# Another order of columns in the large matrix products of a linear-attention and softplus kernel

## The chip, the core and the metric

The kernel runs on one core of one Trainium2 chip. The metric is the device time of one execution in microseconds. Before the change the median of three runs is 870.96 us (868.03 to 871.09).

## What is computed

Eight batches of eight heads of linear attention, 576 positions of 64 elements each, are normalised by their root mean square; the heads are put side by side into rows of 512, and a two-layer network with a softplus between its layers works on the 4608 rows.

```python
kv = np.einsum('bhsd,bhse->bhde', k, v)
out = np.einsum('bhsd,bhde->bhse', q, kv)
rms = np.sqrt(np.mean(out * out, axis=-1, keepdims=True) + 1e-06)
x = (out / rms * g_norm)             # rows of 4608 x 512
h = x @ w_in                         # 512 x 2048
g = np.maximum(h, 0.0) + np.log1p(np.exp(-np.abs(h)))
return g @ w_out                     # 2048 x 512
```

## The kernel before

**Numbers in three parts.** TensorE multiplies operands of the type fp32r. To come nearer to fp32 (the inputs are even wider), each operand is split into a high part, a low part and a third made of the two, and each large product is the sum of three matmuls over these parts. So every factor lies in SBUF as three planes, and the loops over `m` in the products run over them.

**TensorE, banks and columns.** A matmul holds a 128x128 block of one operand (the weight load, PEld in the profile) and streams the other past it, column by column; the result is added up in a bank of PSUM (128 partitions of 512 fp32 numbers). The streamed operand is `rhs` in the code, the bank the first argument. In before, both are walked from their first column to their last.

**The work in order.** First the attention: `kv_of` (L691) forms the 64x64 products, `rows` (L715) applies them to q, squares, sums, takes the root (L719, L723) and scales (L727), and transposes the result (L733, L771 for q). The rows go to memory as `x`, and are read again and split (`split`, L635 to L641). Weights are fetched, converted and split by `weight`, `divide` and `split_weight` (L496 to L524). Then, in two manners, the network:

- *Steps* (`step`): the tokens lie in 12 blocks of 384. For each block `n`, 4 (blocks 0 to 3) or 6 (blocks 4 to 11) chunks `c` of 128 of the 2048 inner columns are done this way, 64 steps. `mm1` (L858) makes 12 matmuls of 384 columns, a softplus and a split follow on ScalarE (L880, L882) and VectorE (L869 and the next), and `mm2` (L865) makes 9 matmuls of 512 columns into the sums of three banks.
- *Wide steps* (`wide_step`): the rest of the inner columns, in pairs of chunks, with the tokens in 9 blocks of 512, in two phases: 27 steps in the first (three for each block) and 21 in the second (three for each of blocks 0 to 2, two for each of blocks 3 to 8), 48 in all. The first layer is done as seven products of sums and differences of quarter matrices instead of eight. Each product (`product`, L1060) makes 6 matmuls of 256 columns into half a bank; ScalarE copies intermediate sums from half bank to half bank (L1101, L1105), and a VectorE addition (L1109) and softplus (L1087) follow. A split on ScalarE and VectorE (L1117, L1120, L1123) makes the input of `mm2` (L1130): 24 matmuls of 512 columns for each step, in four banks.

Partial results of each phase leave through ScalarE (L925) to memory; in the second phase VectorE adds them into the banks again (L904) before the last products are added there.

**What sets the order.** Every piece of work is a task with an engine, an assumed duration, what it comes after, and which buffers it takes and gives back. `Plan.order` simulates the engines with these durations and writes the tasks down in the order that it finds; each engine then runs its own list in that order. Durations in the plan are constants, so they don't follow from a matmul's access pattern. While TensorE has nothing to do early on, the plan inserts spare matmuls (`warm`, L1224), which multiply the identity by itself; their streamed operand is one 128-column block, read four times:

```python
nc.tensor.matmul(new(s, [P, 4, P]), lhsT=ident_r, rhs=ident_r.unsqueeze(1).to_broadcast([P, 4, P]),
                 start=True, stop=True)
```

Two VectorE operations that the prediction uses turn 32x32 blocks: L746 writes its 512 columns contiguously, and L814 writes runs of 32, the next 96 further on, where three tiles share a buffer.

Of the kernel before, what the change touches and what calls it, by code (L numbers as in the profile page):

```python
# [9 lines left out]
F32R = mybir.dt.float32r  # L10
# [8 lines left out]
P = 128  # L19
# [2 lines left out]
DOWN = 1.0 - 2.0 ** -13  # L22
DOWN_G = 1.0 - 0.99 * 2.0 ** -13
E = 1.0 / RADIX


def shaped(x, shape, dtype):
# [28 lines left out]
class Plan:  # L56
# [19 lines left out]
    def slot(self, ring):  # L76
        return Slot(ring)

    def add(self, engine, ns, run, after=(), pos=0.0, take=(), give=(), size=0, behind=None, follows=None, kind="all"):
        pos, behind = round(pos, 4), None if behind is None else round(behind, 4)  # L80
        t = Task(engine, ns, run, [a for a in after if a is not None], pos, list(take), list(give), size)
        for s in t.give:
            s.readers += 1
        self.tasks.append(t)
        t.follows = follows
        t.behind = behind
        t.kind = kind
        return t
# [113 lines left out]
def kernel(  # L202
# [24 lines left out]
    nc = tc.nc  # L227
# [20 lines left out]
    LAST = 2  # L248
# [53 lines left out]
    pieces = sb.tile([P, 12, PIECE], F32R, name="pieces")  # L302
# [183 lines left out]
    def split_weight(w, part_of, n, dst, ready, pos, of_in, by_pe=False):  # L486
# [28 lines left out]
        def third():  # L515
            nc.scalar.activation(dst.tile[:, 2], d.tile, func=AF.Copy, scale=-E / (1.0 + E))

# [5 lines left out]
        def third_of_bank():  # L523
            nc.scalar.activation(dst.tile[:, 2], bank.tile, func=AF.Copy, scale=-E / (1.0 + E))  # L524

# [318 lines left out]
    def step(s):  # L844
        n, c = ORDER[s]
        cs = CHUNKS[n]
        h, g, gv = slot("h"), slot("g"), slot("gv")
        if c == cs[0]:
            sums[:] = [slot(f"s{i}") for i in range(TB)]
        xv, w_in, w_out = xv_slots[n], w_slots[0, c], w_slots[1, c]  # L850
        mine = list(sums)
        kept = c >= 4

        def mm1():
            hp = new(h, [P, NT])
            for m in range(3 * KD):
                i, kd = divmod(m, KD)
                nc.tensor.matmul(hp, lhsT=w_in.tile[:, i, kd * P:(kd + 1) * P], rhs=xv.tile[:, i, kd],  # L858
                                 start=(m == 0), stop=(m == 3 * KD - 1))

        def mm2(i):
            if c == cs[0]:
                new(mine[i], [P, d_model])
            for m in range(3):
                nc.tensor.matmul(mine[i].tile, lhsT=gv.tile[:, m, i * P:(i + 1) * P], rhs=w_out.tile[:, m],  # L865
                                 start=(c == cs[0] and m == 0), stop=(c == cs[-1] and m == 2))

        def low():
            nc.vector.tensor_tensor(out=gv.tile[:, 1], in0=g.tile, in1=gv.tile.bitcast(F32)[:, 0], op=ALU.subtract)  # L869

        def less():
            f32 = gv.tile.bitcast(F32)
            nc.vector.scalar_tensor_tensor(out=gv.tile[:, 2], in0=f32[:, 1], scalar=-RADIX, in1=f32[:, 0],
                                           op0=ALU.mult, op1=ALU.add)

        a = add("PE", 2100, mm1, x_split[n] + factors_done[0, c] + [m for _, m in mm1s[-1:]] +
                (factors_done[1, ORDER[s - 2][1]] if s > 1 else []), s, [h],
                ([xv] if c == cs[-1] else []) + ([w_in] if s == last_step[c] and c != 4 else []))
        mm1s.append((s, a))
        a = add("ACT", 490, lambda: nc.scalar.activation(new(g, [P, NT]), h.tile, func=AF.Softplus, scale=1.0 + E),  # L880
                [a], s, [g], [h])
        a = add("ACT", 530, lambda: nc.scalar.activation(new(gv, [P, 3, NT], F32R)[:, 0], g.tile, func=AF.Copy, scale=DOWN),  # L882
                [a], s, [gv])
        a = add("DVE", 570, low, [a], s, [], [g])
        a = add("DVE", 570, less, [a], s)
        for i in range(TB):
            a2 = add("PE", 700, lambda i=i: mm2(i), [a] + factors_done[1, c] + [mm2s.get(i)], s + 1.5,
                     [mine[i]] if c == cs[0] else [],
                     [gv] + ([w_out] if s == last_step[c] and not kept else []))
            mm2s[i] = a2  # L890
            if c == cs[-1]:
                leave(0, n * TB + i, mine[i], a2, s + 1.5)
# [145 lines left out]
    def wide_step(k):  # L1038
        ph, n, p = STEPS[k]
        ab, gv = slot("ab"), slot("gvp")  # L1040
        b = starts[k]
# [3 lines left out]
        mine = list(wide_sums)  # L1045
        outs = [w_slots[1, c] for c in (2 * p, 2 * p + 1)]

        def place(q):
            return ab.tile[:, q // 2, q % 2 * HW:(q % 2 + 1) * HW]
# [3 lines left out]
        def product(u, q):  # L1053
            f, i = PRODUCTS[u]
            w = forms[p][f].tile
            dst, v = unit_slots[ph, n, u]
            for m in range(3):
                for kd in range(2):
                    at = i * 2 * P + kd * P
                    nc.tensor.matmul(place(q), lhsT=w[:, m, at:at + P], rhs=dst.tile[:, m, v, kd] if u < 6 else dst.tile[:, m, kd],  # L1060
                                     start=(u == 0 and not m and not kd), stop=(m == 2 and kd == 1), skip_group_check=True)

        def multiply(u, q, after, pos, take=(), follows=None):
            f = PRODUCTS[u][0]
            give = [unit_slots[ph, n, u][0]] if last else []
            if final and u in (2, 3, 5, 6):
                give.append(forms[p][f])
            return add("PE", 710, lambda: product(u, q), unit_done[ph, n, u] + forms_done[p][f] + list(after), pos, take, give,
                       follows=follows)
# [3 lines left out]
        def gt(dtype=F32):  # L1073
            if dtype not in held:
                held[dtype] = sb.tile([P, 2, WIDE], dtype, tag=f"g{gv.place}", name=f"g{gv.place}_{dtype == F32}")
            return held[dtype]

        def gvt(m, dtype=F32):
            y = gv.tile[:, m]
            return y if dtype == F32R else y.bitcast(F32)  # L1080
# [5 lines left out]
        def softplus(dst, src):  # L1086
            nc.scalar.activation(dst, src, func=AF.Softplus, scale=1.0 + E)  # L1087

        def begin():
            new(ab, None)  # L1090
            product(0, X)
# [33 lines left out]
        def mm2(c, i):  # L1125
            fresh = first and not c and ph < LAST
            if fresh:
                new(mine[i], [P, d_model])
            for m in range(3):
                nc.tensor.matmul(mine[i].tile, lhsT=(gvt(m, F32R) if m < 2 else gt(F32R))[:, c, i * P:(i + 1) * P], rhs=outs[c].tile[:, m],  # L1130
                                 start=fresh and not m, stop=(last and c == 1 and m == 2), skip_group_check=True)

        seeds = {}
# [19 lines left out]
        for c in range(2):  # L1153
            for i in range(TW):
                slot_pos = b + PACE + MM2[TW * c + i]
                a2 = add("PE", 700, lambda c=c, i=i: mm2(c, i),
                         [split_done[c]] + factors_done[1, 2 * p + c] + ([seeds[i]] if i in seeds and not c else []) +
                         ([before[i]] if c or not first else []), slot_pos, [mine[i]] if first and not c and ph < LAST else [], [gv] + ([outs[c]] if final else []))
                before[i] = a2
                if last and c:  # L1160
                    leave(ph, TW * n + i, mine[i], a2, slot_pos)
# [3 lines left out]
    def whole_scale(pos):  # L1165

        if not wide:
            scale_done.append(add("DVE", 60, lambda: nc.vector.memset(scale, 1.0 + E), (), pos))
            return
# [5 lines left out]
        scale_done.append(add("ACT", 200, lambda: nc.scalar.activation(  # L1175
            scale, total.tile[:, 0, :1], func=AF.Copy, scale=(1.0 + E) * 2.0 ** -30 / (P * 2 * KF * d_model)), [a], pos, [], [total]))

# [82 lines left out]
```

## Time and profile before

| what | value |
|---|---|
| median of three runs (lowest, highest) | 870.96 us (868.03, 871.09) |
| span of the profiled execution, first to last instruction | 867.5 us |
| TensorE busy | 853.9 us, 98%, 6464 matmuls |
| VectorE busy | 704.4 us, 81% |
| ScalarE busy | 521.3 us, 60% |
| GpSimd busy | 76.6 us, 9% |
| DMA queue of the loads and stores | 64.5% of 16 engines' span |
| granted TensorE clock, mean | 1.000 |

For the profiled execution the profile gives the span; its own device time isn't listed apart from the three runs. In the profile, PE is TensorE's matmuls and PEld its weight loads, DVE is VectorE, ACT ScalarE, POOL GpSimd and SP the engine that issues most DMAs. The 40 digits of a slice view are tenths of a fortieth of the span. The chain that ended last is followed back from the last instruction to whatever released each step, or to the instruction ahead of it on its engine. L numbers are lines of the kernel before; `banks<-pieces,gv` names what is written and what is read. The length of one matmul includes the time in which the next one already runs, so matmuls in a row follow each other faster than their mean length says.

### The profile page before, as it was taken

Reading aid. Unit: us, or ns where it says so; the run is one execution under the profiler, and the core shown is the slowest. Engines: PE = TensorE matmul, PEld = TensorE weight load, DVE = VectorE, ACT = ScalarE, POOL = GpSimd, SP = SyncE. Lnnn points to the kernel's source line nnn. Section 1 sums busy time; section 2 is a strip of 40 time slices with the busy share of each in tenths; the row PEclk is TensorE's granted clock in tenths of the full one; section 3 lists DMA queues with packets and bytes.
Section 4 is the critical chain, followed back from the end, with each engine's and each line's share of the span. In section 5 each row is a group of like instructions: output and inputs, shape, how many; then the busy total and the mean of one; then the engine's idle time right before and its main releaser. Section 6 shows DMA issues by size and latency. Waiting matters only on the chain.

```text
span 867.5 us, 17041 instructions
## 1 busy us (share of the span) xinstructions
PE 853.9 (98%) x6464; PEld 760.3 (88%) x6464; DVE 704.4 (81%) x995; ACT 521.3 (60%) x980; POOL 76.6 (9%) x79
## 2 busy tenths in 40 slices
PE   7899999999999999999999999999999999999998
PEld 5678888898888999989999999998999899999996
DVE  7888898888788879798887798878788666788873
ACT  6866664445444467766667655654868555566654
POOL 0342223111113200000000000000000000000000
PEclk9999999999999999999999999999999999999999
DMA  9998998779773655436645546545364752777764
GB/s 278 285 242 230 244 262 255 172 224 234 211 188 114 180 175 166 145 108 209 210 156 164 168 151 205 188 144 170 122 201 140 230 165 91 241 236 241 242 190 126
DMA packets 239778, 167.07 MB, mean 193 GB/s; under 512 B 106320, under 2 KB 198736, under 8 KB 239696
## 3 DMA queue, kind: packets, MB, share of 16 engines
q1 hardware_dynamic: 239392, 165.86, 64.5%
q8 instruction: 50, 0.82, 0.4%
q14 instruction: 32, 0.26, 0.1%
q10 hardware_dynamic: 304, 0.13, 0.1%
HBM read 112.98 MB, written 52.95 MB: 191 GB/s over the span
## 4 chain that ended last, share of the span: by engine, by line
PE 94%; DVE 1%; ACT 1%; POOL 0%; issue 0%; ACTq 0%; DVEq 0%
PE banks L1130 31%; PE banks L1060 28%; PE banks L865 16%; PE banks L858 15%; PE banks L715 2%; PE banks L691 2%; PE banks L733 0%; DVE units L638 0%; DVE half L727 0%; PE banks L1224 0%; POOL roots L723 0%; DVE units L641 0%; DVE roots L719 0%; DVE m L459 0%; ACT units L635 0%
## 5 line engine op out<-in xcount | busy, mean ns | idle before, releaser
L1130 PE MATMUL banks<-pieces,gv 128*128 128x512 f32 x768 | 239.9, 394 | 0.0
L1130 PEld LDWEIGHTS banks<-pieces,gv 128*128 128x128 f32 x768 | 133.5, 189 | 18.4
L1130 PE MATMUL banks<-pieces,g_False 128*128 128x512 f32 x384 | 149.4, 389 | 0.0
L858 PE MATMUL banks<-units,pieces 128*128 128x384 f32 x768 | 145.4, 337 | 0.0
L865 PE MATMUL banks<-pieces,gv 128*128 128x512 f32 x576 | 144.9, 396 | 0.0
L858 PEld LDWEIGHTS banks<-units,pieces 128*128 128x128 f32 x768 | 135.5, 188 | 4.8
L865 PEld LDWEIGHTS banks<-pieces,gv 128*128 128x128 f32 x576 | 106.1, 188 | 20.3
L1060 PEld LDWEIGHTS banks<-units,pieces 128*128 128x128 f32 x840 | 112.8, 190 | 6.8 <-ACT banks L1105 0.4
L1060 PE MATMUL banks<-units,pieces 128*128 128x256 f32 x840 | 117.1, 282 | 0.0
L880 ACT ACTIVATE half<-banks 128x384 f32<-128x384 f32 x64 | 31.4, 491 | 98.2 <-PE banks L858 98.0
L1120 DVE TENSOR_TENSOR gv<-g_True,gv 128x1024 fp32r<-128x1024 f32 x47 | 57.5, 1223 | 37.8 <-ACT gv L1117 37.8
L1130 PEld LDWEIGHTS banks<-pieces,g_False 128*128 128x128 f32 x384 | 72.2, 188 | 15.9
L1060 PEld LDWEIGHTS banks<-units,w 128*128 128x128 f32 x504 | 67.8, 190 | 3.9 <-ACT banks L1105 0.2
L1060 PE MATMUL banks<-units,w 128*128 128x256 f32 x504 | 70.7, 282 | 0.0
L723 POOL TENSOR_TENSOR roots<-roots,half 128x8 f32<-128x8 f32 x36 | 62.3, 1731 | 3.0
L1123 DVE SCALAR_TENSOR_TENSOR g_False<-gv 128x1024 fp32r<-128x1024 f32 x47 | 57.6, 1225 | 1.5
L1109 DVE TENSOR_TENSOR g_True<-banks,g_True 128x512 f32<-128x512 f32 x48 | 33.1, 690 | 30.5 <-PE banks L1060 24.5
L1087 ACT ACTIVATE g_True<-banks 128x256 f32<-128x256 f32 x96 | 36.6, 382 | 32.8 <-PE banks L1060 32.2
L1023 DVE TENSOR_TENSOR units<-loads,units 128x1024 fp32r<-128x1024 f32 x42 | 51.2, 1219 | 6.3 <-ACT units L1020 6.3
L925 ACT ACTIVATE m<-banks 128x512 f32<-128x512 f32 x72 | 42.1, 595 | 19.8 <-PE banks L1130 13.8
L1026 DVE SCALAR_TENSOR_TENSOR units<-units 128x1024 fp32r<-128x1024 f32 x42 | 51.4, 1224 | 1.8
L869 DVE TENSOR_TENSOR gv<-half,gv 128x384 fp32r<-128x384 f32 x64 | 35.4, 553 | 20.6 <-ACT gv L882 19.9
(115 smaller groups left out, 1260.5 us busy)
## 6 DMA issues: line engine op xcount, KB each, us to landing
loads<-x SPq DMA_DIRECT2D x180, 128.0 KB, 2.6
part<-m SPq DMA_DIRECT2D x72, 256.0 KB, 2.9
m<-part SPq DMA_DIRECT2D x72, 256.0 KB, 3.2
loads<-form SPq DMA_DIRECT2D x45, 256.0 KB, 3.2
form<-loads SPq DMA_DIRECT2D x36, 256.0 KB, 3.0
raw<-in_moe_w_in_dram SPq DMA_DIRECT2D x16, 512.0 KB, 4.5
loads<-in_k_dram SPq DMA_DIRECT2D x32, 256.0 KB, 4.1
loads<-in_v_dram SPq DMA_DIRECT2D x32, 256.0 KB, 4.4
```

The costliest lines, as they stand in the source:

```text
L723: nc.gpsimd.tensor_tensor(out=r.tile, in0=r.tile, in1=half, op=ALU.pow)
L858: nc.tensor.matmul(hp, lhsT=w_in.tile[:, i, kd * P:(kd + 1) * P], rhs=xv.tile[:, i, kd], start=(m == 0), stop=(m == 3 * KD - 1))
L865: nc.tensor.matmul(mine[i].tile, lhsT=gv.tile[:, m, i * P:(i + 1) * P], rhs=w_out.tile[:, m], start=(c == cs[0] and m == 0), stop=(c == cs ...
L869: nc.vector.tensor_tensor(out=gv.tile[:, 1], in0=g.tile, in1=gv.tile.bitcast(F32)[:, 0], op=ALU.subtract)
L925: a = add("ACT", 690 if ph == LAST else 600, lambda: nc.scalar.activation(new(ot, [P, d_model]), bank.tile, func=AF.Copy, scale=scale if p ...
L1023: nc.vector.tensor_tensor(out=part_of(1, F32R), in0=xl.tile if m > 1 else xl.tile[:, 0], in1=part_of(0), op=ALU.subtract)
L1026: nc.vector.scalar_tensor_tensor(out=part_of(2, F32R), in0=part_of(1), scalar=-RADIX, in1=part_of(0), op0=ALU.mult, op1=ALU.add)
L1060: nc.tensor.matmul(place(q), lhsT=w[:, m, at:at + P], rhs=dst.tile[:, m, v, kd] if u < 6 else dst.tile[:, m, kd], start=(u == 0 and not m ...
L1087: nc.scalar.activation(dst, src, func=AF.Softplus, scale=1.0 + E)
L1120: nc.vector.tensor_tensor(out=gvt(1, F32R), in0=gt(), in1=gvt(0), op=ALU.subtract)
L1123: nc.vector.scalar_tensor_tensor(out=gt(F32R), in0=gvt(1), scalar=-RADIX, in1=gvt(0), op0=ALU.mult, op1=ALU.add)
L1130: nc.tensor.matmul(mine[i].tile, lhsT=(gvt(m, F32R) if m < 2 else gt(F32R))[:, c, i * P:(i + 1) * P], rhs=outs[c].tile[:, m], start=fresh ...
```

## The change

A new function gives a view of an operand in which the columns come in another order. Its number `k` picks the order: 0 leaves it as it is.

```diff
+def woven(x, k):
+    def pieces(w, q):
+        return x.rearrange("p (q j w) -> p j q w", q=q, w=w)
+    def blocks(w):
+        return x.rearrange("p (b w) -> p b w", w=w)
+    if k == 1:
+        return pieces(32, 2)
+    if k == 2:
+        return pieces(64, 2)
+    if k == 3:
+        return blocks(128)[:, ::-1]
+    if k == 4:
+        return pieces(16, 4)
+    if k == 5:
+        return x[:, ::-1]
+    if k == 6:
+        return x.rearrange("p (b e w) -> p b e w", e=2, w=64)[:, :, ::-1]
+    if k == 7:
+        return pieces(32, 2)[:, ::-1]
+    if k == 8:
+        return blocks(16)[:, ::-1]
+    if k == 9:
+        return blocks(64)[:, ::-1]
+    if k == 10:
+        return x.rearrange("p (b e w) -> p b e w", e=2, w=16)[:, :, ::-1]
+    if k == 11:
+        return pieces(8, 2)
+    return x
```

`pieces(w, q)` cuts the columns into `q` equal parts and takes `w` columns of each in turn. `blocks(w)[:, ::-1]` takes blocks of `w` columns from the last to the first. Orders 6 and 10 exchange neighbouring runs of 64 and of 16 columns. Order 5 goes from the last column to the first, one at a time; it is the only one in which columns inside a run are turned round.

The four large products use it with the number of their block, for the streamed operand and for the bank alike, so that each column of the result lies where it lay before:

```diff
-                nc.tensor.matmul(hp, lhsT=w_in.tile[:, i, kd * P:(kd + 1) * P], rhs=xv.tile[:, i, kd],
+                nc.tensor.matmul(woven(hp, n), lhsT=w_in.tile[:, i, kd * P:(kd + 1) * P], rhs=woven(xv.tile[:, i, kd], n),
...
-                nc.tensor.matmul(mine[i].tile, lhsT=gv.tile[:, m, i * P:(i + 1) * P], rhs=w_out.tile[:, m],
+                nc.tensor.matmul(woven(mine[i].tile, n), lhsT=gv.tile[:, m, i * P:(i + 1) * P], rhs=woven(w_out.tile[:, m], n),
...
-                    nc.tensor.matmul(place(q), lhsT=w[:, m, at:at + P], rhs=dst.tile[:, m, v, kd] if u < 6 else dst.tile[:, m, kd],
+                    nc.tensor.matmul(woven(place(q), n), lhsT=w[:, m, at:at + P],
+                                     rhs=woven(dst.tile[:, m, v, kd] if u < 6 else dst.tile[:, m, kd], n),
...
+                k = n + 6 if ph == LAST and n in (4, 5) else n
-                nc.tensor.matmul(mine[i].tile, lhsT=(gvt(m, F32R) if m < 2 else gt(F32R))[:, c, i * P:(i + 1) * P], rhs=outs[c].tile[:, m],
+                nc.tensor.matmul(woven(mine[i].tile, k), lhsT=(gvt(m, F32R) if m < 2 else gt(F32R))[:, c, i * P:(i + 1) * P],
+                                 rhs=woven(outs[c].tile[:, m], k),
```

In the steps `n` runs from 0 to 11, in the wide steps from 0 to 8; `mm2` of the second phase uses orders 10 and 11 for its blocks 4 and 5. The held operand, the number of matmuls, the number of columns of each and the constants of the plan are the same.

## The prediction

> **What bounds the kernel now.** I read the page first: busy shares, slices, the chain that ended last, the groups.
>
> ```profile
> PE 853.9 (98%) x6464; PEld 760.3 (88%) x6464; DVE 704.4 (81%) x995; ACT 521.3 (60%) x980; POOL 76.6 (9%) x79
> PE   7899999999999999999999999999999999999998
> PEclk9999999999999999999999999999999999999999
> ...
> PE 94%; DVE 1%; ACT 1%; POOL 0%; issue 0%; ACTq 0%; DVEq 0%
> PE banks L1130 31%; PE banks L1060 28%; PE banks L865 16%; PE banks L858 15%; PE banks L715 2%; PE banks L691 2%; PE banks L733 0%; DVE units L638 0%; DVE half L727 0%; PE banks L1224 0%; POOL roots L723 0%; DVE units L641 0%; DVE roots L719 0%; DVE m L459 0%; ACT units L635 0%
> ```
>
> TensorE is busy in all but 13.6 us of the 867.5 us span, at the full granted clock (the view by cores gives 1.000), and the chain runs along it nearly everywhere. The four lines that the change edits, L858, L865, L1060 and L1130, are 90% of the chain. So whatever happens to the rate of these matmuls is paid or gained one for one.
>
> "Mean ns of one" (394 for a 128x512 matmul) is no price, since matmuls overlap. The chain in order of time tells how fast they follow each other:
>
> ```profile
> 111.74 4.35 PE banks L865 x18
> ...
> 124.27 4.18 PE banks L858 x24
> 128.45 4.12 PE banks L865 x18
> ...
> 417.86 2.87 PE banks L1060 x24
> ```
>
> The columns are start, length, place and count. 4.12 us / 18 = 228.9 ns for 512 columns, 4.18 / 24 = 174.2 ns for 384, 2.87 / 24 = 119.6 ns for 256. Each 128 columns add 54.6 or 54.7 ns, so a column costs 0.427 ns, and 119.6 - 256 x 0.427 leaves 10.3 ns that a matmul pays whatever its width. The edited lines issue 768 x 384 + 576 x 512 + 2016 x 256 + 1152 x 512 = 1,695,744 columns in 4512 matmuls: 724 + 46 = 770 us, 89% of the span, which agrees with the 90% above.
>
> The view of TensorE's waits says what is left: none is longer than 1.7 us, and all those it lists stand at other lines (L691, L1224, L771, L715, L521, L733), mostly in the opening.
>
> **The change, part by part.**
>
> *What stays.* The listing of both kernels' instructions, engine by engine, has the same instructions in the same order on all five engines; on TensorE each wait has the same semaphore and value as before. No matmul, weight load, byte or column is added or taken away. What differs is the pattern in which 4032 of the 4512 matmuls walk their moving operand and their bank, both with the same pattern. 480 keep the plain order: those of block 0 (48 at L858, 36 at L865, 252 at L1060, 144 at L1130).
>
> *Reordered columns, read side.* By the length of the contiguous ascending runs, the columns split into 175,104 plain; 152,064 in runs of 128; 400,896 of 64; 345,600 of 32; 396,288 of 16; 79,872 of 8; and 145,920 with no ascending run at all, where k = 5 walks backward one element at a time (block 5: 72 x 384 + 54 x 512 + 210 x 256 + 72 x 512). The runs are 53,004 in 3624 matmuls, so 49,380 hops stand inside matmuls. TensorE has one row of before with such hops: the spare matmuls of L1224 read one block of 128 four times over, a hop back after each 128.
>
> ```profile
> 43.29 1.08 PE L1224 MATMUL banks<-ident_r 128*128 128x512 f32 x4
> ```
>
> Four starts span 1.08 less the last one's own 0.39 (its length alone, as the timeline has it elsewhere): 0.69 / 3 = 230 ns, against 228.9 with no hop. Three hops cost 1 ns or nothing. That is the nearest row, so I take 0 for a hop. From above, a farther row: VectorE's transposes of 128x512 take 707 ns at L814, which writes 32-element runs 96 apart, and 685 at L746, which writes contiguously; 22 ns over 15 hops is 1.5 ns. At that price 49,380 hops are 74 us.
>
> *Write side.* No matmul of before writes its bank in another order than ascending, so the trace has no row. Below: nothing, since the same columns go to the same bank. A gain is bounded by the fixed 10.3 ns: 4032 x 10.3 = 42 us if the new order hid all of it. Above: a write stream at half rate costs another 0.427 ns per column. I take 0, by L1224's row again, whose hops cost the same engine nothing.
>
> [...]
>
> *Backward step.* No row of any engine here has a step of minus one. [...] I take 0, since the L1224 row is the only one of this engine, but of all zeros in this sum this one is the weakest.
>
> *Waits that moved.* On ScalarE 33 of the 48 copies of L1105 wait for an earlier ScalarE instruction as well. That instruction stands several places ahead in the same queue, so it is long over; what remains is one more wait instruction, 17 ns by ScalarE's own in the view of L880: 33 x 17 = 0.6 us on an engine that is 60% busy. Behind the copy stand TensorE's products of L1060. They are covered by what TensorE does meanwhile: at 396.13 us the copy runs under six matmuls of L1130 (1.39 us in the chain). Where that cover is thin, the view of L1060 has three waits for L1105, 0.6 us in all; 17 ns on each is 0.05 us. On VectorE 11 instructions name other semaphores for the same order, and six wait instructions fewer are issued; VectorE is not on the chain there. I count nothing for either.
>
> *Sum.* 0 + 0 + 0 + 0.05 us on 867.5. The page gives only the span of the profiled execution; the three runs stand at 868.03 to 871.09 us, 0.5 to 3.6 us above it, with a median of 870.96. I predict the median: **871.0 us**.
>
> **The rivals.**
>
> 1. *The backward block runs at half rate.* [...] For it: nothing in the trace excludes it. [...] Price 62 us: 871 + 62 = 933. This is the case on the other side, with one place: block 5, between 165 and 197, 507 and 554, and 739 and 760 us of the span. It decides from 0.03 ns per backward element on (4.4 us / 145,920). Chance 0.20.
> 2. *Each hop costs a little,* on the write side if not on the read side. At VectorE's 1.5 ns this gives 871 + 74 = 945; at 0.3 ns, 886. From 0.09 ns per hop (4.4 us / 49,380) it is slower. Against it stand L1224's three hops. Chance 0.13.
> 3. *A bank that isn't written straight through is written at half rate,* whatever its runs. All but the 175,104 plain columns pay 0.427 ns more: 1,520,640 x 0.427 = 649 us, so 1520. Nothing in the trace shows it, and L1224 speaks against it for reading only. Chance 0.07. [...]
> 4. *The new order hides part of the fixed 10.3 ns,* down to 829. It would need that part to hang on where one matmul ends and the next begins; it is the same at all three widths, and no row shows it otherwise. Chance 0.08.
>
> That the change does nothing, because the patterns are simplified away, is excluded: the listing shows 128x8x2x32 where 128x512 stood.
>
> **How the numbers follow.** No cost 0.52, the rivals 0.20, 0.13, 0.07 and 0.08. A measurement of this kernel can tell about 0.5%, 4.4 us, from no change. No cost is "within 0.5%": 0.52. Rivals 1 to 3 are slower: 0.40. Rival 4 is faster: 0.08. The likeliest case alone spans 867 to 874. The range for 8 in 10 takes in the half rate of the backward block and the dear hops: 865 to 945. It leaves out rival 3, most of rival 4 and a quarter rate backward.
>
> **What would show it.** Right: in the chain, 24 products of L1060 at 2.87 us, 18 of L865's at 4.12 and 24 of L858's at 4.18 in every block (the lines move down by 33 or more). Rival 1: the same, except in block 5, where a 512-column matmul takes 447 ns and a 256-column one 229. Rival 2: the spacing grows with the number of runs, most in block 11 (runs of 8), least in block 3 (runs of 128). Rival 3: all blocks but 0 near 447 ns. Rival 4: under 226 ns for 512 columns. My weakest step is the zero for a direction and for written hops, for which before has no row; it fails if a matmul's rate is set by how its bank is written.

## The result and the profile after

The changed kernel takes **877.29 us** (median of three runs, 877.19 to 877.33) against 870.96 us: a ratio of 1.0087, 95% interval 1.006 to 1.0115. It is slower by 0.6 to 1.15%. The prediction's likeliest case, no change, didn't come; the time lies inside its range. The profiled execution has a span of 875.5 us, against 867.5 before, in a run of 877.29 us: 1.8 us lie around the span.

The page of the changed kernel, its busy times and the chain that ended last (the lines have moved: L891, L898, L1093 and L1165 are L858, L865, L1060 and L1130 of before):

```profile
span 875.5 us, 17069 instructions
PE 861.0 (98%) x6464; PEld 763.0 (87%) x6464; DVE 704.8 (81%) x995; ACT 521.0 (60%) x980; POOL 76.8 (9%) x79
...
PE 94%; DMA 2%; DVE 1%; ACT 1%; issue 1%; SPq 0%; POOL 0%; DVEq 0%; ACTq 0%
PE banks L1165 30%; PE banks L1093 27%; PE banks L898 16%; PE banks L891 15%; PE banks L748 2%; PE banks L724 2%; DMA raw<-in_moe_w_in_dram 1%; DMA loads<-in_v_dram 1%; PE banks L1260 1%; PE banks L766 0%; SPq L794 0%; DVE units L671 0%; DVE half L760 0%; PE banks L804 0%; POOL roots L756 0%
```

TensorE is busy for 7.1 us more, with as many matmuls as before; VectorE and ScalarE are as they were. So TensorE's own matmuls became slower. Adding up the times from each matmul's start to the next one's start in the two traces gives the account:

| matmuls | before, us | after, us |
|---|---|---|
| 384 columns (steps) | 136.7 | 138.8 |
| 512 columns (steps) | 136.1 | 137.9 |
| 512 columns (wide steps) | 264.9 | 268.4 |
| 256 columns (products) | 240.5 | 240.0 |
| all others | 83.6 | 84.8 |

The edited lines gained 6.9 us of the span's 8.0. Another 1.2 us is in the other matmuls, most of it in the first 45 us. There the changed kernel's execution had a stretch of 3.4 us at a granted clock of 0.50 (26.3 to 29.7 us), but that isn't needed for it: the run below that only reads in another order has 1.00 there and 84.7 us in these matmuls. That part varies between executions, from 83.2 to 85.8 us in the traces of the runs below in which these matmuls are as in before.

The chain by blocks tells which orders pay. The changed kernel in block 9 (blocks of 64 columns, backward) and block 11 (halves by turns in runs of 8):

```profile
292.02 4.12 PE banks L898 x18
296.14 2.10 PE banks L891 x12
...
348.88 2.20 PE banks L891 x12
351.08 4.38 PE banks L898 x18
```

and the kernel before in its block 11:

```profile
350.88 2.10 PE banks L858 x12
352.98 4.13 PE banks L865 x18
```

Block 9, with hops, costs what before costs: 4.12 us for 18 matmuls of 512 columns, 229 ns each. Block 11 takes 4.38 us, 243 ns each, and at 384 columns 183 instead of 175 (2.20 and 2.10 us for 12). The backward block 5:

```profile
191.04 2.13 PE banks L891 x12
193.18 2.10 PE banks L898 x9
```

2.13 / 12 = 177.5 ns and 2.10 / 9 = 233 ns. Over all its matmuls the block pays 2 to 4 ns more than before, far from half rate.

### The profile page after: what moved, and what is told of

It is laid out like the page before. It is cut to its first block, busy times and chain, and to the rows that moved or that the text cites. A ratio compares the mean times of both kernels' runs of the same rounds, so it can differ in the third digit from the quotient of the medians.

```text
span 875.5 us, 17069 instructions
## 1 busy us (share of the span) xinstructions
PE 861.0 (98%) x6464; PEld 763.0 (87%) x6464; DVE 704.8 (81%) x995; ACT 521.0 (60%) x980; POOL 76.8 (9%) x79
## 4 chain that ended last, share of the span: by engine, by line
PE 94%; DMA 2%; DVE 1%; ACT 1%; issue 1%; SPq 0%; POOL 0%; DVEq 0%; ACTq 0%
PE banks L1165 30%; PE banks L1093 27%; PE banks L898 16%; PE banks L891 15%; PE banks L748 2%; PE banks L724 2%; DMA raw<-in_moe_w_in_dram 1%; DMA loads<-in_v_dram 1%; PE banks L1260 1%; PE banks L766 0%; SPq L794 0%; DVE units L671 0%; DVE half L760 0%; PE banks L804 0%; POOL roots L756 0%
## 5 line engine op out<-in xcount | busy, mean ns | idle before, releaser
L1165 PE MATMUL banks<-pieces,gv 128*128 128x512 f32 x768 | 241.8, 396 | 0.0
L1165 PE MATMUL banks<-pieces,g_False 128*128 128x512 f32 x384 | 151.6, 395 | 0.0
L1165 PEld LDWEIGHTS banks<-pieces,gv 128*128 128x128 f32 x768 | 133.3, 189 | 19.6
L891 PE MATMUL banks<-units,pieces 128*128 128x384 f32 x768 | 147.5, 341 | 0.0
L898 PE MATMUL banks<-pieces,gv 128*128 128x512 f32 x576 | 146.8, 399 | 0.0
L891 PEld LDWEIGHTS banks<-units,pieces 128*128 128x128 f32 x768 | 137.1, 188 | 5.1
L898 PEld LDWEIGHTS banks<-pieces,gv 128*128 128x128 f32 x576 | 106.5, 188 | 21.6
L1093 PEld LDWEIGHTS banks<-units,pieces 128*128 128x128 f32 x840 | 112.4, 189 | 7.3 <-ACT banks L1139 0.4
L1093 PE MATMUL banks<-units,pieces 128*128 128x256 f32 x840 | 116.8, 282 | 0.0
L1165 PEld LDWEIGHTS banks<-pieces,g_False 128*128 128x128 f32 x384 | 72.2, 188 | 17.2
L1093 PEld LDWEIGHTS banks<-units,w 128*128 128x128 f32 x504 | 67.6, 189 | 4.3 <-ACT banks L1139 0.2
L1093 PE MATMUL banks<-units,w 128*128 128x256 f32 x504 | 70.5, 282 | 0.0
```

What stands on the lines that cost most here:

```text
L891: nc.tensor.matmul(woven(hp, n), lhsT=w_in.tile[:, i, kd * P:(kd + 1) * P], rhs=woven(xv.tile[:, i, kd], n), start=(m == 0), stop=(m == 3 ...
L898: nc.tensor.matmul(woven(mine[i].tile, n), lhsT=gv.tile[:, m, i * P:(i + 1) * P], rhs=woven(w_out.tile[:, m], n), start=(c == cs[0] and m ...
L1093: nc.tensor.matmul(woven(place(q), n), lhsT=w[:, m, at:at + P], rhs=woven(dst.tile[:, m, v, kd] if u < 6 else dst.tile[:, m, kd], n), star ...
L1165: nc.tensor.matmul(woven(mine[i].tile, k), lhsT=(gvt(m, F32R) if m < 2 else gt(F32R))[:, c, i * P:(i + 1) * P], rhs=woven(outs[c].tile[:, ...
```

## Experiments: which side pays, and for what

A hop, as in the prediction, is a step inside a matmul to a column that isn't the next one; a run is what lies between two hops.

**Theories.** First: the streamed operand's read pays when its runs are short. Rival: the write to the bank pays. Second rival: any hop pays, however long its run.

### Reading alone and writing alone

Both edits are made in the changed kernel.

```diff
 e_read
-nc.tensor.matmul(woven(mine[i].tile, n), ..., rhs=woven(w_out.tile[:, m], n),
+nc.tensor.matmul(mine[i].tile, ..., rhs=woven(w_out.tile[:, m], n),
 e_write
-nc.tensor.matmul(woven(mine[i].tile, n), ..., rhs=woven(w_out.tile[:, m], n),
+nc.tensor.matmul(woven(mine[i].tile, n), ..., rhs=w_out.tile[:, m],
```

The other three matmuls are edited in the same way.

> Only the streamed operand is read in the orders of the change; the banks are written straight through, so the columns of the products land in other places. In the trace of the changed kernel the edited lines gained 6.9 us over before, and no block ran at half rate: blocks with runs of 64 or more gained nothing, and those with shorter runs up to 16 ns a matmul (block 11 at the 512-column line of the steps: about 243 ns a matmul against about 229). If the reading pays: the whole gain stays, 1.006 to 1.011 of before, and block 11 keeps about 243 ns. If the writing pays: before's time within 0.3%, and block 11 near 229. If both sides pay a part each: between, 1.003 to 1.005.

> Only the banks are written in the orders of the change; the streamed operand is read straight through, so the columns of the products land in other places. If the reading pays: before's time within 0.3%, and block 11 at the 512-column line of the steps near 229 ns. If the writing pays: 1.006 to 1.011 of before and block 11 near 243 ns. If the cost stands where one matmul ends and the next begins in the bank (a price of each matmul, not of each hop): the backward block keeps its 233 ns and block 11 loses most of its own.

Reading alone: 877.16 us, 1.0083 of before (1.0069 to 1.0097), the whole loss. Writing alone: 869.29 us, 0.9997 (0.9988 to 1.0007). The chain in block 11, first of reading alone:

```profile
348.81 2.20 PE banks L891 x12
351.00 4.38 PE banks L898 x18
```

and of writing alone:

```profile
350.53 2.10 PE banks L891 x12
352.63 4.13 PE banks L898 x18
```

The first has the lengths of the changed kernel, the second those of before: in every block but the first two the medians are within 1 ns. Here the banks were written backward, and in runs of 8, for nothing.

So rival 3 of the prediction, half rate for a bank that isn't written straight through, falls: 0.9997, and 4.13 us for 18 matmuls in block 11, as before. Every order written here goes in runs of at least 8 or straight backward, so shorter runs in the bank aren't tested by this run.

### Long runs only

In the changed kernel, the backward order and every order with runs under 64 columns is exchanged for one with runs of 64 or 128:

```diff
+    k = {1: 2, 4: 2, 5: 3, 7: 9, 8: 9, 10: 6, 11: 2}.get(k, k)
```

> The changed kernel with each order that has runs under 64 columns, and the backward one, exchanged for one with runs of 64 or more; hops, backward blocks and exchanged neighbours stay, and the result is the reference's. If the length of the run decides: before's time, 0.997 to 1.003. If any hop or any departure from the plain order pays: over 1.004.

869.50 us, 1.0004 of before (0.9995 to 1.0013). The chain in block 11, with halves by turns in runs of 64 (L892 and L899 are the lines of 384 and 512 columns):

```profile
351.69 2.10 PE banks L892 x12
353.79 4.13 PE banks L899 x18
```

Hops, backward blocks and exchanged neighbours cost nothing when 64 columns or more stand together. Hops as such are not the price; L1224's row, which the prediction leant on, has runs of 128 and could show no more than that.

### Is it a collision with the weight load?

Nearly every weight load of these four lines starts 2 to 5 ns after a matmul starts and takes 188 to 192 ns in the median, so the load of one operand runs beside the stream of the other. Two runs, edited from the changed kernel, test whether that is what the dear orders meet.

```diff
 e_narrow
-woven(mine[i].tile, n), lhsT=gv.tile[:, m, i * P:(i + 1) * P], ...
+woven(mine[i].tile[:32], n), lhsT=gv.tile[:, m, i * P:i * P + 32], ...
 e_one_weight
+woven(mine[i].tile, n), lhsT=gv.tile[:, 0, :P], ...
```

Both do the same in the wide steps. The first also fills the banks with zeros at the start.

> The changed kernel with only 32 columns of the held operand in the 512-column matmuls (of steps and wide steps): each weight load reads a quarter as many columns, each matmul fills 32 of 128 partitions, and the rest of each sum is left out (zero from one fill at the start). The streamed reads are those of the changed kernel. If the dear orders collide with the weight load: the differences between blocks shrink to a quarter, block 11 from 15 ns over block 0 to 4 or less, and the plain blocks come nearer to 219 ns. If the orders are dear to the streamed read alone: block 11 stays 12 to 16 ns above block 0, as before.

> The changed kernel, but every 512-column matmul loads the same 128 columns of its held operand (the first, of the high part) instead of walking through them: the weight load is as wide as before and always from one place, the streamed reads are those of the changed kernel, and the low and third parts of the held operand are left out of the sums. With a narrower load the dear orders had kept their price. If the price hangs on where the weight load reads: some block of the 512-column matmuls moves by 3 ns or more, and the plain blocks lose their alternation between 224 and 236 ns. If the streamed read alone makes it: every block within 1 ns of the changed kernel (block 0 near 231, block 11 near 242).

The narrow version takes 880.7 us (a single run; its first matmul starts 4.6 us later than in the changed kernel). The weight load fell from 188 ns (106.5 us busy in 576) to 108 ns:

```profile
L898 PEld LDWEIGHTS banks<-pieces,gv 128*32 128x32 f32 x576 | 61.4, 108 | 60.5
```

and block 11 stayed dear:

```profile
354.92 4.38 PE banks L898 x18
```

So it did with one weight for all, a single run of 876.27 us:

```profile
350.10 4.38 PE banks L898 x18
```

With one weight every block's mean at 512 columns is within 0.5 ns of the changed kernel's. With the narrow load the blocks' medians at 512 columns moved by 3 ns at most, up or down, and block 11 of the steps not at all: it stands 10 ns above block 0 there, 11 in the changed kernel, a little under the foretold 12 to 16. Plain block 0 of the wide steps went from 230.2 to 231.0 ns in the mean, no nearer to 219. So the collision with the weight load, as these expectations put it, falls: neither the load's width nor the place it reads makes the price. A collision that hangs on when each load comes isn't excluded, since no run leaves the weight loads out.

### Many orders side by side

`woven` takes a kind, a width and a number of parts, and each block has its own order. "Halves by turns, runs of 8" is `pieces(8, 2)` of the change, quarters are `pieces(8, 4)`; "turned round" reverses the order of the runs in each group. In both runs, and in all that follow, operand and bank are walked in the same order, as in the change.

> Nine orders side by side for the products of 256 columns, and twelve for the 384-column matmuls of the steps; all 512-column matmuls are plain. Products, blocks 0 to 8: blocks of 8 backward; halves by turns in runs of 16 and 8; quarters by turns in runs of 8; neighbours of 8 and of 4 exchanged; blocks of 4 and of 2 backward; halves by turns in runs of 4. The 384-column matmuls, blocks 0 to 11: plain; 32 backward; 32 exchanged; 8 exchanged; 8 backward; 4 backward; 4 exchanged; eighths by turns in runs of 16; quarters by turns in runs of 2; 1 backward; 16 backward; quarters by turns in runs of 4. If the fixed 10 to 13 ns of a matmul are collisions of its read with the weight load, some order should come under the 118 ns that blocks of 16 backward gave (112 to 117), since the stream alone needs 256 x 0.427 = 109 ns. If 118 is the floor, all nine stand between 118 and 125, and short runs at the upper end.

> Many orders side by side, to find what the read pays for. Steps, blocks 0 to 11, at 384 and 512 columns: neighbours of 2 exchanged; groups of four runs of 4 turned round; quarters by turns in runs of 8; eighths by turns in runs of 4; neighbours of 4 exchanged; halves by turns in runs of 4 and of 2; neighbours of 8 exchanged; quarters by turns in runs of 4 and of 2; blocks of 4 backward; neighbours of 1 exchanged. 512 columns of the wide steps, blocks 0 to 8: neighbours of 4 exchanged; 8 backward; neighbours of 2 exchanged; eighths by turns in runs of 16; quarters in runs of 8 taken eighth by eighth; groups of four runs of 4 turned; sixteenths by turns in runs of 4; groups of eight runs of 4 turned; and 32 parts by turns in runs of 4. [...] If each hop costs a fixed time: neighbours of 1 and 2 exchanged would be dearest, over 255.

In two places the runs differ from these texts: block 11 of the first has quarters by turns in runs of 8, not of 4, at 384 columns, and block 4 of the second's wide steps has eighths by turns in runs of 4. The second also has an order for each block of the products. Turns in runs of 1 weren't measured, so they aren't in the table.

Between them (single runs, 886.15 and 939.4 us) and the changed kernel, the traces give medians from one start to the next, in ns; a dash is an order not run at that width. Orders not listed lay at 239 or less at 512 columns.

| order | 512 | 384 | 256 |
|---|---|---|---|
| plain (before) | 227 to 233 | 174 | 120 |
| runs of 64 and more (after) | 228 to 233 | 174 | 119 to 120 |
| halves by turns, runs of 32 (after) | 236 to 237 | 180 | 119 to 120 |
| halves by turns, runs of 8 | 242 | 184 | 122 |
| one by one backward | 233 | 176 | 118 |
| neighbours of 8 exchanged | 267 | 200 | 133 |
| neighbours of 4 exchanged | 231 to 236 | 173 to 180 | 113 to 120 |
| neighbours of 2 exchanged | 227 to 230 | 174 | 120 |
| neighbours of 1 exchanged | 227 | 174 | 120 |
| blocks of 8 backward | 234 to 235 | 178 | 120 |
| groups of four runs of 4 turned round | 266 to 267 | 200 | 133 |
| quarters by turns, runs of 8 | 232 | 174 | 119 |
| halves by turns, runs of 4 | 254 | 191 | 127 |
| quarters by turns, runs of 4 | 265 | 177 | 134 to 135 |
| eighths by turns, runs of 4 | 276 | 174 | 121 |
| 16ths by turns, runs of 4 | 247 | - | 114 to 115 |
| 32nds by turns, runs of 4 | 225 | - | - |
| halves by turns, runs of 2 | 333 | 251 | - |
| quarters by turns, runs of 2 | 443 | 335 | - |

At 256 columns one and the same order gave 113 to 120 (neighbours of 4), so differences under 7 ns there can't be put down to the order alone.

The chain of the second run, in its block 9 (quarters by turns, runs of 2) and in block 11 (neighbours of 1 exchanged); L879 and L886 are its lines of 384 and 512 columns:

```profile
340.16 3.99 PE banks L886 x9
344.16 4.03 PE banks L879 x12
...
399.88 2.10 PE banks L879 x12
401.99 4.13 PE banks L886 x18
```

What follows. Whether reading or writing pays for runs under 8 isn't shown, since both sides hop here; below, the price is that of the order. *A fixed price for each hop falls:* neighbours of 1 exchanged hops the most and costs nothing (227 and 174 ns). *Nor does the length of the run decide alone:* runs of 2 cost nothing where neighbours are exchanged (227 to 230 ns at 512 columns), and half or all of the stream again where they go far before they come back (333 by halves, 443 by quarters; 251 and 335 at 384). *The distance of the hop counts:* with runs of 4, hops of 256 bytes (eighths at 512 columns, quarters at 256), of 512 (quarters at 512, halves at 256) and of 1024 (halves at 512) cost 7 to 46 ns a matmul; of 64 bytes (32nds at 512, 16ths at 256), they save 3 to 6. Hops of 128 bytes cost 18 ns at 512 columns (16ths) and 1 at 256 (eighths).

### Can an order be faster?

> The kernel before, with only the products of 256 columns in order 8 (blocks of 16 columns, from the last to the first) in every block of the wide steps. In the changed kernel these products were 1.3 to 1.4 ns a matmul faster in this order (block 8) than before. If that is a real gain of these matmuls: 2016 x 1.3 = 2.6 us less, 0.997 of before. If it was given by the neighbours in the stream (the 512-column matmuls in the same order behind them): within 0.1% of before. If short runs cost there too once all are in that order: over 1.001.

Edited from the kernel before, products only:

```diff
 e_prod8
-nc.tensor.matmul(place(q), ..., rhs=dst.tile[:, m, v, kd] ...
+nc.tensor.matmul(woven(place(q), 8), ..., rhs=woven(dst.tile[:, m, v, kd] ..., 8),
```

866.93 us, 0.9965 (0.9952 to 0.9979): a small real gain, from a kernel in which nothing but the order of the products' columns differs. A group of its products (L1093):

```profile
419.62 2.84 PE banks L1093 x24
```

That is 118 ns each, and it is the read's gain: block 8 of the wide steps, which has this order in the changed kernel, has a median of 118 ns with the reading alone and 120 with the writing alone. Neighbouring runs of 4 were the better order for the products. The chain of the first run with many orders, in block 4 (neighbours of 8 exchanged) and then block 5 (neighbours of 4); L1079 is its line of the products, L1150 that of the 512 columns behind them:

```profile
498.08 3.20 PE banks L1079 x24
...
530.96 2.72 PE banks L1079 x24
533.68 2.72 PE banks L1150 x12
```

3.20 / 24 = 133 ns, 2.72 / 24 = 113 ns; and the plain 512-column matmuls behind the latter take 2.72 / 12 = 227 ns, without the slow ones (228 to 236 ns) with which most groups of before begin. Four versions put that order everywhere, or only beside plain 512-column matmuls, or mix it with hops of 64 bytes:

```diff
 e_swap4        neighbouring runs of 4 exchanged in all four lines
 v_prod_swap4   the same at 256 and 384 columns; 512 plain
 v_hop64        runs of 4 with hops of 64 bytes in all four lines:
                ("turns", 4, 16) at 256, ("turns", 4, 24) at 384, ("turns", 4, 32) at 512
 v_mix          neighbouring runs of 4 at 256 and 384; hops of 64 bytes at 512
```

> All four large matmuls, in all blocks, read and write with neighbouring runs of 4 columns exchanged; the result is the reference's. In the run with nine orders for the products this order gave 113 to 114 ns at 256 columns against 120 in the plain order, and 173 ns at 384 columns from the second matmul on, where the plain order needs 175 to 185 for the first six. If the gain belongs to the order: the products give 2016 x 5.4 = 10.9 us, the 384-column matmuls about 1.5 us, and the 512-column matmuls up to 1728 x 9 = 16 us if they lose the same part of the 13 ns that stand above their stream: 0.968 to 0.987 of before. If it was a matter of the neighbours in that run (plain 512-column matmuls behind): under 4 us, over 0.995.

> Neighbouring runs of 4 columns exchanged in the products of 256 columns and in the 384-column matmuls of the steps; the 512-column matmuls plain. With this order everywhere the products fell only to 114 to 120 ns, while beside plain 512-column matmuls one block of them stood at 113 to 114 throughout, and the plain matmuls behind it lost 2.5 ns as well. If a matmul's cost hangs on how its own order meets that of the matmul in front of it: 2016 x 5.4 + 1152 x 2.5 + 576 x 2 + 768 x 1 = 15.7 us less, 0.980 to 0.985 of before. If the one block was an exception: 0.993 to 1.000, as the version with this order everywhere.

> All four large matmuls take runs of 4 columns, each 16 columns (64 bytes) after the one before, then the next set: sixteenths by turns at 256 columns, 24ths at 384, 32nds at 512. In the run with many orders one block had this order at 256 and 512 columns: 114 to 115 ns against 120, and 225 against 229. If that holds in all blocks: 2016 x 4.5 + 1728 x 4.2 = 16.3 us less, and at 384 columns nothing known (no row): 0.978 to 0.985. If the price of a short run far from the next returns at other addresses: over 0.995.

> Runs of 4 exchanged at 256 and 384 columns, and runs of 4 with hops of 64 bytes at 512 columns. If the gains of the two orders are each their own: 2016 x 5.4 + 1728 x 4.2 = 18 us less, 0.977 to 0.983. If they hang on the neighbour in the stream: another value than the sum of the two other versions' parts, between 0.980 and 1.000.

| version | median, us | ratio to before (95%) |
|---|---|---|
| e_swap4 | 870.49 | 1.0007 (0.9996 to 1.0018) |
| v_prod_swap4 | 854.11 | 0.982 (0.9805 to 0.9834) |
| v_hop64 | 848.36 | 0.9757 (0.974 to 0.9774) |
| v_mix | 860.61 | 0.9893 (0.9876 to 0.9909) |

`v_prod_swap4` came as foretold for the case that a matmul's cost hangs on its surroundings (0.980 to 0.985). The order with hops of 64 bytes beats before by 2.4%, a little more than the 1.5 to 2.2% foretold. Its page and chain (L879, L886, L1081 and L1152 are the four lines):

```profile
span 848.3 us, 17075 instructions
PE 832.4 (98%) x6464; PEld 746.8 (88%) x6464; DVE 703.5 (83%) x995; ACT 521.5 (61%) x980; POOL 76.4 (9%) x79
```

```profile
345.85 2.05 PE banks L879 x12
347.90 4.06 PE banks L886 x18
...
519.56 2.68 PE banks L1152 x12
...
533.79 3.48 PE banks L1081 x30
```

512 columns take 4.06 / 18 = 226 or 2.68 / 12 = 223 ns, 384 take 171, 256 take 3.48 / 30 = 116. TensorE is as full as before (98%) and does the same matmuls in 21.5 us less.

The mixture shows that a matmul's price also hangs on what ran before. The products in exactly the same order take 113 ns in `v_prod_swap4`, 113 to 120 in `e_swap4`, and a median of 120 in `v_mix`; the first expected value of `e_swap4` and the first of `v_mix` were missed for that reason. The matmul just ahead doesn't decide it, as two groups of 24 products in `v_mix` show:

```profile
417.70 2.74 PE banks L1081 x24
...
607.64 2.88 PE banks L1081 x24
```

Both groups have the same order and stand behind three 512-column matmuls of the same order. In the first the products settle at 113 to 114 ns from the fourth on, in the second at 120 from the second on, and each group stays there to its end. So something is carried along from further back; what it is, no run shows. A meeting in time of the streamed read and the weight load would be one candidate: by the expectation of the run with nine orders for the products, a time under 118 ns was its sign, and 113 came.

## Why the prediction came out as it did

- **What bounds the kernel** held: the loss is on TensorE's edited lines, paid one for one, and apart from about 1 us in the opening no wait grew into it.
- **"so I take 0 for a hop"** is the step that failed. It came from the L1224 row, and that row has runs of 128. At that length zero was right: blocks 2, 3, 6 and 9 cost nothing. For runs of 32 and less the term isn't zero: all in all, with the little that the backward block adds, 6.9 us, or 6.9 us / 49,380 = 0.14 ns a hop, between the two bounds of 0 and 1.5 ns. Rival 2 ("each hop costs a little") gave the right size of loss for a small price, but with the wrong law: blocks 4 and 8 have the same number of runs, all of 16 columns, yet at 384 columns block 4 pays 8 ns a matmul in the mean (177.8 to 185.9) and block 8 only 2 (177.7 to 179.5). Here the length of the run and where the hop goes decide, not the number of hops. And it is the read that pays, where the rival had it "on the write side if not on the read side".
- **The range** held partly by luck. Its upper end was set by a half rate of the backward block and by VectorE's price of a hop (933 and 945 us), and neither came; nor did the quarter rate that it leaves out. The case that did come, a small price of short runs, had only the 0.13 of rival 2.
- **The write side's 0** was right, although no row backed it: 0.9997. The half rate of rival 3 was an assumption that no run shows.
- **The backward step's 0** was nearly right, and rival 1 (half rate, 62 us) is out. Its price, 145,920 backward columns at another 0.427 ns each, is a term that no run shows; the block paid 2 to 4 ns a matmul at 384 and 512 columns, and 1 ns less at 256. The block that the prediction feared most is one of the cheaper ones.
- **Rival 4** (part of the fixed 10.3 ns can be hidden) had 0.08 and wasn't what the change did as a whole, but in the products it happened: block 8's went from 120 to 118 ns by the order of the read, and the best order shown takes 21.5 us off TensorE's busy time, half of the 42 us that rival 4 allowed. So the fixed part isn't fixed; it changes with the order of the columns.
- **The moved waits** cost nothing, as counted: 33 wait instructions of 17 ns on ScalarE, and three waits of TensorE's weight loads for that copy, 0.6 us in all, as before.

```profile
L1139 ACTq EVENT_SEMAPHORE  x33: 17/17/17, 401.2 to 857.0; - x33
```

**What stays open.** That the read pays for runs of 8 to 32 is shown; why it does, isn't. For runs under 8 and for the gains of hops of 64 bytes, read and write were never parted. Open too are why a hop of 64 bytes is cheaper than going straight on, why runs of 8 exchanged with their neighbour (267 ns) and groups of four runs of 4 turned round (266 to 267) cost more than blocks of 8 backward (234), and what a group of matmuls carries over from those before it. With runs of 4 by turns, distances of 256, 512, 768 and 1024 bytes are dear (7 to 46 ns a matmul; 768 is halves at 384 columns, 17 ns), but 128 bytes are too at 512 columns (247 ns), and no rule is shown.

## What to carry to other kernels

Where TensorE is the bound, price a matmul by its start-to-start time, not by its length, and see how much of it isn't stream (10.3 ns of 120 here): that rest changed with the order of the columns, and part of it was had back without moving a byte (0.9757 with hops of 64 bytes). What an order gave also hung on the matmuls around it (113 or 120 ns for the same products), so it has to be measured in the whole kernel. Writing the banks in runs of 8 or more and backward cost nothing here (0.9997), so to that extent the bank could follow whatever order the read likes. A zero taken from one row holds for what that row does and no further: runs of 128 say nothing of runs of 8.

## What was unexpected in the hardware

- Plain ascending order isn't the fastest here: runs of 4 with hops of 64 bytes gave 223 to 226 ns instead of 229 at 512 columns and 114 to 116 instead of 120 at 256, 2.4% of the whole kernel.
- Walking operand and bank with neighbouring runs of 8 exchanged cost 11 to 17% (267, 200 and 133 ns at 512, 384 and 256 columns); with single columns exchanged it cost nothing (227, 174 and 120 ns).
- The same matmul in the same order, behind others of the same order, takes 113 or 120 ns, and a whole group of 24 stays at the one or the other.
- The banks were written in runs of 8 or straight backward at the price of the plain order (0.9997).
